# First two tiles' values loaded as two pieces per partition, the memory's rows from GpSimd's queue

## The chip, the cores and the metric

One core of a Trainium2 chip runs the whole program. The metric is device time of one execution in microseconds (us), measured without a profile; the kernel before was run three times, and one more execution was profiled. The engines are named as in the profile: PE (TensorE's matmuls), PEld (its weight loads), DVE (VectorE), ACT (ScalarE), POOL (GpSimd), SP (SyncE, which only issues DMAs here).

## What is computed

Chunked attention with memory rows, and then two dense layers one after the other. Shapes: 4 batches, 8 heads, 768 positions, head width 64; that is 3072 tokens of 512 values; the hidden width is 2048. Inputs and result are float32.

```python
for c in range(24):                       # chunks of 32 queries
    k_ctx = k[:, :, max(0, 32*c-16) : min(S, 32*c+32+8)]
    k_full = concat(mem_k (8 rows), k_ctx);  v_full = concat(mem_v (8 rows), v_ctx)
    a = softmax(q_c @ k_full.T / 8)       # 64 keys for each query
    out[:, :, c] = a @ v_full
x = out as [3072, 512]
h = x @ w_in;   x = (h * clip(h + 3, 0, 6) / 6) @ w_out          # first layer
h = x @ w_in2;  x = (h if h>=1, 0 if h<=-1, else (h+1)**2/4) @ w_out2   # second
```

## The kernel before

**Tiling.** Tokens go in six tiles of 512 (T). Attention goes in 24 value blocks of four chunks (128 queries), s = 0 to 23, so blocks 0 to 3 feed the first tile and 4 to 7 the second. Queries and keys are loaded in blocks of three chunks (j), values per block s as one tile `v_sb` of 128 partitions by 2 by 512 for s < 8: chunk c of the block has partitions 32c to 32c+31, and its 64 value rows (8 of the memory, 56 of the context) lie as rows 0 to 31 in the first half and 32 to 63 in the second. Each dense product is done in three matmuls of 512 columns (high by high, high by low, low by high part), lines L603 to L605 for the hidden product (tile `ph`), L652 to L654 and L657 to L659 for the projection. The weights come packed (`raw`, 512 KB each, issued at L279) and are unpacked by ACT and DVE into `w` (L286 to L312).

**Attention of a block.** Scores on PE (L460), maximum on DVE, exponentials on ACT (L485), normalising and a transpose on DVE (L495, L504), values on PE (L529), and the split of the result into a high part on ACT and a low part on DVE (L575, L579). The hidden products of the first tile read the blocks 0 to 3 whole, so the first `ph` matmul comes after the values of block 3.

**What sets the order.** Nothing is ordered by hand. `Plan.run` (L136) is a list scheduler: every task has a key, a duration table entry (such as `("SP", 430)`), reads, writes and a buffer from a pool; the planner picks the task that can start soonest by its own clock, and within 100 ns of that the one of the lowest key. The instructions are then written out engine by engine in the order of the planned starts, so on the chip each engine runs that fixed list, waiting where an input isn't there. SP's list is the DMA issues.

**Fillers.** Where the plan leaves PE idle before 60 us, lines L752 to L769 put matmuls of the constant `warm` tile (bfloat16) into a buffer that the next task will overwrite anyway:

```python
while at + ns <= t.start + more:
    P.matmul(c, warm, warm[:, :n].unsqueeze(1).to_broadcast([128, m, n]), ...)
    at += ns
```

They have the line L765. How many stand in a gap is decided by the plan's times, with 2.4 columns to the nanosecond; they then run whether or not the gap is there.

**Values' loads.** `load_values` (L385) cuts each block into runs of consecutive rows, one DMA each from SP: about 8 or 9 for each of the blocks 0 to 7, of 8, 24, 32, 64 or 96 rows. For j < NEARLY the source is the array `qkv`, in which queries, keys and values of a block j lie side by side; for later j it is `qk` and `vv`. Each DMA from SP signals on one of eight semaphores in turn, and a DMA waits until the one eight places before it has landed.

Of the kernel before, what the change touches and what calls it, by code (L numbers as in the profile page):

```python
# [22 lines left out]
NMEM = 8  # L23
CHUNK, LEFT, RIGHT = 32, 16, 8
# [7 lines left out]
NC = DM // 128  # L32
NF = DFF // 128
GRP = 4
NEARLY = 6
LATE_W = GRP * (QB + KB)
T = 512
NT = NTOK // T
# [38 lines left out]
class Plan:  # L77
# [58 lines left out]
    def run(self, at):  # L136
        free = dict(at)
        bw = 0
        last_kind = None
        ready = {e: [] for e in free}  # L140

        def put(t):
            for e, _ in t.ways:
                ready[e].append(t)

        for t in self.tasks:
            if not t.left:
                put(t)
        left = len(self.tasks)
        order = []  # L150
        while left:
            best = None
            for e, ts in ready.items():
                found = []
                blocked = set()
                for t in sorted(ts, key=lambda t: (t.key, t.n)) if e == "SP" else ts:
                    est = max(free[e], t.ready)
                    taken = [] if blocked & {p for b in t.bufs if not b.slot for p in b.pools} else self.slots_for(t)
                    if taken is None or len(taken) < sum(b.slot is None for b in t.bufs):
                        if e == "SP":  # L160

                            blocked.update(p for b in t.bufs if b.slot is None for p in b.pools)
                        continue
                    found.append((max([est, *(s.at + HOP for s in taken)]), t))
                if not found:
                    continue
                first = min(x[0] for x in found)
                if e == "PE" and last_kind:

                    same = [x for x in found if x[1].kind and x[0] <= free[e] + WINDOW]  # L170
                    found = same or found
                est, t = min(
                    (x for x in found if x[0] <= first + WINDOW), key=lambda x: (x[1].key, x[1].n)
                )
                if best is None or est < best[0]:
                    best = est, e, t
            assert best, ("no task can start", [
                (t.n, t.emit.__qualname__, t.key, [b.name for b in t.bufs if b.slot is None])
                for ts in ready.values() for t in ts][:20])
            est, e, t = best  # L180
            for x, _ in t.ways:
                ready[x].remove(t)
            ns = dict(t.ways)[e]
            if e == "PE":
                ns += CHANGE * (bool(t.kind) != bool(last_kind))
                last_kind = t.kind
            t.eng, t.start = e, est
            free[e] = est + ns
            t.end = est + ns + TAIL[e]
            if t.kb:  # L190
                bw = max(bw, t.end + 1900) + t.kb / 0.39
                t.end = bw
            for b, s in zip([b for b in t.bufs if b.slot is None], self.slots_for(t)):
                b.slot, s.used = s, True
            for b in t.bufs:
                b.users -= 1
                b.free_at = max(b.free_at, t.end)
                if not b.users:
                    b.slot.used, b.slot.at = False, b.free_at
            for d in t.then:  # L200
                d.left -= 1
                d.ready = max(d.ready, est)
                if not d.left:
                    put(d)
            for d in t.next:
                d.left -= 1

                alone = all(x == e for x, _ in d.ways)
                d.ready = max(d.ready, est + ns if alone else t.end + HOP)
                if not d.left:  # L210
                    put(d)
            order.append(t)
            left -= 1
        order.sort(key=lambda t: (t.start, t.n))
        return order
# [11 lines left out]
def fused_kernel(ctx: ExitStack, tc: tile.TileContext, qkv, qk, vv, wpk, const, out):  # L227
# [40 lines left out]
    def weight(l, f, z, key, after=()):  # L268
# [43 lines left out]
            eng.tensor_tensor(out=t[:, 1], in0=words()[2], in1=t[:, 0], op=ALU.subtract)  # L312

        lo, hi = (raw, "lo"), (raw, "hi")
        add(("SP", 430), key - 4, load, writes=[lo, hi], kb=512, after=after)
        add([("DVE", dve(512, True)), ("ACT", 575)], key - 0.5, shift, writes=[lo])
        add(("ACT", 575), key - 0.5, rebase, writes=[hi])
        add(("DVE", dve(512)), key - 0.4, sign, [hi], [lo])
# [21 lines left out]
    def wide(j):  # L340
        return j * NCH >= 2 * T // CHUNK

    def load_block(j, key):

        early = key < 0

        over = key > 1.75 * NF
        far = 3 * (not early)  # L350
        w = KB + KC if wide(j) else KB
        q = q_buf[j] = Buf(
            ["in"] + ["w"] * ((early or over) and not wide(j)), [128, NP * (QB + w)], F32, "q_sb",
            **({"w": 1} if early else {}),
        )
        if j < NEARLY:
            src = qkv[j, :, :WQ]
        else:
            src = qk[2 * (j - NEARLY):2 * (j - NEARLY) + 2].rearrange("g d w -> (g d) w")
        after = last_w if over else ()  # L360
        if not wide(j):
            add(("SP", 430), key - 6 - far, lambda e: nc.sync.dma_start(tile_of(q), src), writes=[(q, 0)], kb=448, after=after, line="load")
            return
        k4 = lambda: tile_of(q)[:, NP * QB:].rearrange("p (a t) -> p a t", a=NP)
        add(
            ("SP", 430), key - 6 - far, lambda e: nc.sync.dma_start(
                k4()[:, :, :KB], src[:, NP * QB:].rearrange("p (a t) -> p a t", a=NP)
            ), writes=[(q, 1)], kb=256, after=after, line="load",
        )
        add(  # L370
            ("SP", 430), key - 6 - far, lambda e: nc.sync.dma_start(tile_of(q)[:, :NP * QB], src[:, :NP * QB]),
            writes=[(q, 0)], kb=192, after=after, line="load",
        )

        def spread(e):
            k = k4()
            cast(e, k[:, :, KB + NMEM:], k[:, :, NMEM + CHUNK:KC + CHUNK])
            cast(
                e, k[:, :, 2 * CHUNK:2 * CHUNK + 2 * KC].rearrange("p a (b t) -> p a b t", b=2)[:, :, :, :NMEM],
                k[:, :, :NMEM].unsqueeze(2).to_broadcast([128, NP, 2, NMEM]),  # L380
            )

        add([("DVE", 330), ("ACT", 400)], key - 4.5, spread, [], [(q, 1)])

    def load_values(s, key):  # L385
# [4 lines left out]
        v = v_buf[s] = Buf(  # L390
            ["lv"] + ["w"] * early, [128, 2, H * D], F32, "v_sb", **({"w": 1} if early else {}),
        )
        runs = []
        for c in range(NSB):
            j, i = divmod(s * NSB + c, NCH)
            cuts = [0] + [NMEM] * (i > 0) + [CHUNK] * (not late) + [KC]
            for a, b in zip(cuts, cuts[1:]):
                row = a if b <= NMEM else a + CHUNK * i
                p, col = (64 * (c % 2) + a, c // 2) if late else (CHUNK * c + a % CHUNK, a // CHUNK)
                for r in runs:  # L400
                    if r[0] == j and r[1] + r[4] == row and r[2] + r[4] == p and r[3] == col:
                        r[4] += b - a
                        break
                else:
                    runs.append([j, row, p, col, b - a])
        for n, (j, row, p, col, m) in enumerate(sorted(runs, key=lambda r: (r[3], r[2]))):
            if j < NEARLY:
                src, rows = qkv[j, row:row + m, WQ:], lambda t: t
            else:
                g = 2 * (j - NEARLY)  # L410
                src, rows = vv[g:g + 2, row:row + m, :].rearrange("g k c -> k g c"), lambda t: t.rearrange("k (g c) -> k g c", g=2)
            add(
                ("SP", 430), key - 5 - 3 * (not early),
                lambda e, src=src, rows=rows, p=p, m=m, col=col: nc.sync.dma_start(rows(tile_of(v)[p:p + m, col]), src),
                writes=[(v, n)], kb=2 * m, line="load v",
            )
        v.parts = len(runs)

    def block(s, key):
        first = key < 0  # L420
# [89 lines left out]
        def values(e, m=None):  # L510
# [23 lines left out]

        qs = sorted({j for j, _ in places})
        add(
            ("PE", 750 if all(wide(j) for j in qs) else 1450), key - 4, scores,
            [(q_buf[j], x) for j in qs for x in range(1 + wide(j))],
            [(sc[0], 0), (sc[1], 0)], hold=[st], line="scores", kind="a",
        )  # L540
# [6 lines left out]
            add(("ACT", 1150), key - 3, lambda e, h=h: exps(e, h), [(sc[h], 0), (sm, 2)], [(st, h), (sm, 0, h)])  # L547
        add(("DVE", 280), key - 2.5, weigh, [(sm, 0, 0), (sm, 0, 1)], [(sm, 3)])
        add(("DVE", dve(512)), key - 2.4, norm, [(sm, 3)], [(st, 0), (st, 1)])
        of_v = [(v, n) for n in range(v.parts)]  # L550
        if late:
            for c in chunks:
                for b in range(2):
                    add(("DVE", dve(256)), key - 2.2, lambda e, c=c, b=b: turn_part(e, c, b), [(st, 0), (st, 1)], [(tr, c, b)])
            ts = [(tr, c, b) for c in chunks for b in range(2)]
            add(("PE", 750), key - 1, values, [*ts, *of_v], [(x, 0) for x in pv], line="values", kind="a")
        else:
            add(("DVE", 635), key - 2.2, turn, [(st, 0), (st, 1)], [(tr, 0)])
            for m in range(2):
# [128 lines left out]
    def second_x(n):  # L688
        xhi, xlo = xbuf[NT + n]
        key = NK + NF * n  # L690
        for c in range(NC):
            x = Buf(["in", "o", "st"], [128, T], F32, "x2raw")
            add(
                ("SP", 430), key - 8 + 0.5 * c, lambda e, c=c, x=x: nc.sync.dma_start(tile_of(x), ymid[n, :, c]),
                [("ymid", n, c)], [(x, 0)], kb=256, after=[h_tasks[key - NF]],
            )
            ways = [("ACT", act(T)), ("DVE", dve(T, True))]
# [138 lines left out]
```

## Time and profile before

| | us |
|---|---|
| median of 3 runs | 1161.72 (1161.0 to 1162.23) |
| the profiled execution, its own time | 1161.94 |
| its span, first to last instruction | 1160.1 |
| PE busy in the span | 1144.1 |
| DVE, ACT, POOL busy | 614.9, 457.8, 0.2 |

The time of an execution holds 1.84 us that lie outside the span. PE is busy nearly throughout, and what it does after the first tile's attention is a fixed list of matmuls; the first 60 us look different. In the trace a float32 matmul counts as two (the order has 64 for the values of a block, the trace 128). A wait is put down to what ended it; "issue" means that the engine waited for nothing that the profile shows.

### The profile page before, as it was taken

To read this page: it belongs to the slowest core of one execution; us is meant where nothing else is said; L and a number is where in the kernel's file an instruction comes from. 1 tells how busy PE (TensorE), PEld (TensorE's weight loads), DVE (VectorE), ACT (ScalarE), POOL (GpSimd) and SP (SyncE) were. 2 spreads that over 40 slices of the span, in tenths; PEclk is the share of its full clock that TensorE was granted. 3 is DMA by queue.
4 is the path that set the end of the run, shared out by engine and by line. 5 is a ranking of instruction groups with operands and counts; after the bars stand their busy time and mean duration, and the time that the engine had idled before them with its cause. 6 is when DMAs were issued, how large, how long until landed. Compare 5 with 4: busy or idle time off the path is not lost.

```text
span 1160.1 us, 20860 instructions
## 1 busy us (share of the span) xinstructions
PE 1144.1 (99%) x8766; PEld 939.5 (81%) x8766; DVE 614.9 (53%) x1116; ACT 457.8 (39%) x1083; POOL 0.2 (0%) x4
## 2 busy tenths in 40 slices
PE   8899999999999999999999999999999999999998
PEld 6687888888887888888888888888888888888887
DVE  2589955445555445643899634434434434433433
ACT  3599633334333333333788423223223223222221
POOL 0000000000000000000000000000000000000000
PEclk8699999999999999999999999999999999999999
DMA  6791131112112112210656300200200200000100
GB/s 207 249 396 55 57 100 35 51 54 90 48 35 87 51 51 74 70 38 19 200 183 216 91 1 1 73 1 1 73 1 1 73 1 1 37 1 1 37 1 37
DMA packets 48644, 81.05 MB, mean 70 GB/s; under 512 B 5158, under 2 KB 28582, under 8 KB 48550
## 3 DMA queue, kind: packets, MB, share of 16 engines
q1 hardware_dynamic: 48550, 79.71, 20.9%
q8 instruction: 69, 1.13, 0.4%
q14 instruction: 25, 0.20, 0.1%
HBM read 67.11 MB, written 12.58 MB: 69 GB/s over the span
## 4 chain that ended last, share of the span: by engine, by line
PE 97%; DMA 1%; issue 1%; ACT 1%; DVE 0%; SPq 0%; DVEq 0%; ACTq 0%
PE ph L603 15%; PE ph L604 15%; PE ph L605 15%; PE py L652 8%; PE po L657 8%; PE po L659 8%; PE po L658 8%; PE py L653 7%; PE py L654 7%; PE sc L460 2%; PE pv L529 2%; PE pv L519 1%; PE pv L765 1%; DMA ymid<-ysb 0%; DMA v_sb<-qkv 0%
## 5 line engine op out<-in xcount | busy, mean ns | idle before, releaser
L603 PE MATMUL ph<-xhi,w 128*128 128x512 f32 x768 | 300.5, 391 | 0.0
L604 PE MATMUL ph<-xlo,w 128*128 128x512 f32 x768 | 299.2, 390 | 0.0
L605 PE MATMUL ph<-xhi,w 128*128 128x512 f32 x768 | 299.0, 389 | 0.0
L626 ACT ACTIVATE r<-r,bias 128x512 f32<-128x512 f32 x96 | 69.3, 722 | 286.6 <-DVE r L623 286.6
L633 DVE TENSOR_TENSOR glo<-r,ghi 128x512 fp32r<-128x512 f32 x192 | 132.6, 690 | 81.9 <-ACT ghi L632 80.4
L632 ACT CAST ghi<-r 128x512 fp32r<-128x512 f32 x192 | 119.5, 623 | 133.7 <-DVE r L629 71.2
L603 PEld LDWEIGHTS ph<-xhi,w 128*128 128x128 f32 x768 | 144.5, 188 | 30.5 <-ACT raw L286 0.3
L605 PEld LDWEIGHTS ph<-xhi,w 128*128 128x128 f32 x768 | 144.3, 188 | 30.2
L604 PEld LDWEIGHTS ph<-xlo,w 128*128 128x128 f32 x768 | 144.5, 188 | 29.7
L652 PE MATMUL py<-ghi,w 128*128 128x512 f32 x384 | 153.5, 400 | 1.3 <-DVE ysb L679 1.3
L654 PE MATMUL py<-ghi,w 128*128 128x512 f32 x384 | 149.8, 390 | 0.0
L653 PE MATMUL py<-glo,w 128*128 128x512 f32 x384 | 149.8, 390 | 0.0
L657 PE MATMUL po<-w,ghi 128*128 128x512 f32 x384 | 149.4, 389 | 0.0
L658 PE MATMUL po<-w,ghi 128*128 128x512 f32 x384 | 149.4, 389 | 0.0
L659 PE MATMUL po<-w,glo 128*128 128x512 f32 x384 | 149.4, 389 | 0.0
L619 DVE SCALAR_TENSOR_TENSOR r<-r,ph 128x512 f32<-128x512 f32 x96 | 65.8, 685 | 154.0 <-ACT r L616 153.3
L623 DVE TENSOR_SCALAR r<-ph 128x512 f32<-128x512 f32 x96 | 66.3, 691 | 152.2 <-PE ph L605 152.2
L616 ACT ACTIVATE r<-ph,bias 128x512 f32<-128x512 f32 x96 | 66.2, 689 | 191.9 <-PE ph L605 191.9
L629 DVE TENSOR_TENSOR r<-ph,r 128x512 f32<-128x512 f32 x96 | 66.3, 690 | 74.7 <-ACT r L626 74.7
L652 PEld LDWEIGHTS py<-ghi,w 128*128 128x128 f32 x384 | 72.0, 188 | 18.4 <-DVE ysb L679 1.7
L654 PEld LDWEIGHTS py<-ghi,w 128*128 128x128 f32 x384 | 72.1, 188 | 15.2
L659 PEld LDWEIGHTS po<-w,glo 128*128 128x128 f32 x384 | 72.1, 188 | 15.0
(52 smaller groups left out, 962.7 us busy)
## 6 DMA issues: line engine op xcount, KB each, us to landing
raw<-wpk SPq DMA_DIRECT2D x64, 512.0 KB
ymid<-ysb SPq DMA_DIRECT2D x24, 256.0 KB
x2raw<-ymid SPq DMA_DIRECT2D x24, 256.0 KB
out<-osb SPq DMA_DIRECT2D x24, 256.0 KB
q_sb<-qk SPq DMA_DIRECT2D x21, 256.0 KB
v_sb<-vv SPq DMA_DIRECT2D x43, 112.0 KB
q_sb<-qk SPq DMA_DIRECT2D x21, 192.0 KB
v_sb<-vv SPq DMA_DIRECT2D x24, 128.0 KB
```

The lines of the kernel that those rows point to most:

```text
L603: P.matmul(p, whi[:, c, :], xh[:, c, :], start=(c == 0), stop=False)
L604: P.matmul(p, whi[:, c, :], xl[:, c, :], start=False, stop=False)
L605: P.matmul(p, wlo[:, c, :], xh[:, c, :], start=False, stop=(c == NC - 1))
L626: add(("ACT", act(T) + 100), k + 0.35, lambda e: A.activation(out=rt(), in_=rt(), func=AF.Square, bias=bias[:, 1:2], scale=0.5,), [], [(r, ...
L632: add(("ACT", act(T)), k + 0.5, lambda e: A.copy(tile_of(ghi), rt()), [(r, 0)], [(ghi, 0)])
L633: add(("DVE", dve(T)), k + 0.6, lambda e: V.tensor_tensor(out=tile_of(glo), in0=rt(), in1=tile_of(ghi), op=ALU.subtract,), [(r, 0), (ghi, ...
L652: P.matmul(y, w2hi, gh, start=first, stop=False)
L653: P.matmul(y, w2hi, gl, start=False, stop=False)
L654: P.matmul(y, w2lo, gh, start=False, stop=last)
L657: P.matmul(y, gh[:, t], wt[:, 0], start=first, stop=False)
L658: P.matmul(y, gh[:, t], wt[:, 1], start=False, stop=False)
L659: P.matmul(y, gl[:, t], wt[:, 0], start=False, stop=last)
```

## The change

The values of blocks 0 to 7 are loaded with one DMA for each chunk whose memory rows and context rows lie next to each other in the source (the first chunk of a block j: 32 partitions, two pieces of 512 values each), and with two for the others: 24 partitions with two pieces from SP, and 8 partitions (the memory's rows and eight context rows) with two pieces from GpSimd's queue. NEARLY goes from 6 to 11, so that all of these blocks are read from `qkv`. Besides, numbers in the planner's tables change: 430 to 450 for a DMA issue from SP, 800 for a later value load (whose key keeps its place), 750 to 800 for later scores, 750 to 1070 for later values, 337 to 450 for a partial transpose, and a rule for the landing of a DMA from GpSimd.

```diff
-NEARLY = 6
+NEARLY = 11
@@ Plan.run
             if t.kb:
                 bw = max(bw, t.end + 1900) + t.kb / 0.39
-                t.end = bw
+                t.end = bw if e == "SP" else t.end + 1900 + t.kb / 0.1
@@ load_values
+        if not late:
+            v.parts = []
+            for c in range(NSB):
+                j, i = divmod(s * NSB + c, NCH)
+                for a, b, row, step, way in (
+                    ((0, CHUNK, 0, CHUNK, ("SP", 500)),) if i == 0 else (
+                        (NMEM, CHUNK, CHUNK * i + NMEM, CHUNK, ("SP", 500)),
+                        (0, NMEM, 0, CHUNK * (i + 1), ("POOL", 550)),
+                    )
+                ):
+                    rows = qkv[j, row:row + b - a, WQ:]
+                    src = bass.AP(rows.tensor, rows.offset, [rows.ap[0], [step * rows.ap[0][0], 2], rows.ap[1]])
+                    part = (v, c, a)
+                    v.parts.append(part)
+                    add(
+                        way, key - 5, lambda e, src=src, p=CHUNK * c + a, n=b - a:
+                        (nc.gpsimd if e == "POOL" else nc.sync).dma_start(tile_of(v)[p:p + n], src),
+                        writes=[part], kb=5.6 * (b - a), line=way[0] + "load v",
+                    )
+            return
-            cuts = [0] + [NMEM] * (i > 0) + [CHUNK] * (not late) + [KC]
+            cuts = [0] + [NMEM] * (i > 0) + [KC]
-                ("SP", 430), key - 5 - 3 * (not early),
+                ("SP", 800), key - 8,
@@ block
-            ("PE", 750 if all(wide(j) for j in qs) else 1450), key - 4, scores,
+            ("PE", 800 if all(wide(j) for j in qs) else 1450), key - 4, scores,
-                    add(("DVE", dve(256)), key - 2.2, lambda e, c=c, b=b: turn_part(e, c, b), [(st, 0), (st, 1)], [(tr, c, b)])
+                    add(("DVE", 450), key - 2.2, lambda e, c=c, b=b: turn_part(e, c, b), [(st, 0), (st, 1)], [(tr, c, b)])
-            add(("PE", 750), key - 1, values, [*ts, *of_v], [(x, 0) for x in pv], line="values", kind="a")
+            add(("PE", 1070), key - 1, values, [*ts, *of_v], [(x, 0) for x in pv], line="values", kind="a")
```

SP's list at the program's start, of the kernel before: the first two blocks of queries and keys (`q_sb`), the values of block 0 (`v_sb`), and the third `q_sb`.

```order
L362 DMA q_sb<-qkv 128x896 x2
L414 DMA v_sb<-qkv 32x512
L414 DMA v_sb<-qkv 8x512
L414 DMA v_sb<-qkv 24x512
L414 DMA v_sb<-qkv 8x512
L414 DMA v_sb<-qkv 24x512
L414 DMA v_sb<-qkv 32x512
L414 DMA v_sb<-qkv 96x512
L414 DMA v_sb<-qkv 32x512
L362 DMA q_sb<-qkv 128x896
```

The same place of the changed kernel:

```order
L363 DMA q_sb<-qkv 128x896 x2
L412 DMA v_sb<-qkv 32x2x512
L412 DMA v_sb<-qkv 24x2x512 x2
L412 DMA v_sb<-qkv 32x2x512
L363 DMA q_sb<-qkv 128x896
```

Eight issues of values became four; two pieces of 8 partitions went to POOL's list, which holds 21 such DMAs in all and nothing else. The first `raw` is the 41st DMA of SP's list before and the 23rd now.

SP's list of the kernel before from the last values of block 3 on: the first packed weights (`raw`), the next `q_sb`, and the values of block 4.

```order
L414 DMA v_sb<-qkv 96x512
L414 DMA v_sb<-qkv 32x512
L279 DMA raw<-wpk 128x512 x2
L362 DMA q_sb<-qk 128x896
L279 DMA raw<-wpk 128x512 x2
L414 DMA v_sb<-qkv 8x512
L414 DMA v_sb<-qkv 24x512
```

The same place of the changed kernel:

```order
L412 DMA v_sb<-qkv 24x2x512 x2
L412 DMA v_sb<-qkv 32x2x512
L280 DMA raw<-wpk 128x512 x2
L363 DMA q_sb<-qkv 128x896
L280 DMA raw<-wpk 128x512 x6
L363 DMA q_sb<-qkv 128x896
L280 DMA raw<-wpk 128x512 x2
L412 DMA v_sb<-qkv 24x2x512 x2
L412 DMA v_sb<-qkv 32x2x512
L412 DMA v_sb<-qkv 24x2x512
L280 DMA raw<-wpk 128x512 x6
```

Ten weight loads now stand ahead of the values of block 4 where four stood, and six more between these and block 5's. Block 4's values go into the buffer of block 0's, block 5's into that of block 1's, in both kernels.

PE's list of the kernel before around the values of block 0 (L529; L765 are fillers, L460 the scores of block 2):

```order
L765 MATMUL pv<-warm 128x128
L765 LDWEIGHTS warm
L765 MATMUL pv<-warm 128x128
L529 MATMUL pv<-tr,v_sb 64x32 x64
L460 MATMUL sc<-q_sb 32x8 x6
L460 MATMUL sc<-q_sb 32x56 x2
```

The same place of the changed kernel (L552 are the values of block 0; the scores ahead of them, L483, are those of block 2):

```order
L483 MATMUL sc<-q_sb 32x64 x2
L483 MATMUL sc<-q_sb 32x56 x4
L552 MATMUL pv<-tr,v_sb 64x32 x64
L788 LDWEIGHTS warm
L788 MATMUL sc<-warm 128x256
```

The scores run one block further ahead, and the fillers stand in other gaps. Counted over the lists, up to and just behind the first `ph` matmul, whose place among the real work is the same (five blocks of scores and four of values stand ahead of it):

| fillers (columns each) | before | now |
|---|---|---|
| ahead of scores 0 | 26 (256) | 27 (256) |
| ahead of scores 1 | 15 (256) | 16 (256) |
| other gaps, up to values 3 | 11 (256), 145 (128) | 47 (256), 7 (128) |
| ahead of the first `ph` | 8 (512) | 10 (512) |
| behind the first 12 `ph` matmuls | 17 (256) | 15 (512) |

PE's list after the values of block 7 is the same in both kernels.

## Rows read from the trace of the kernel before

**Rows 1.** The page: engines' busy time, and the queue of kind "instruction".

```profile
PE 1144.1 (99%) x8766; PEld 939.5 (81%) x8766; DVE 614.9 (53%) x1116; ACT 457.8 (39%) x1083; POOL 0.2 (0%) x4
...
q8 instruction: 69, 1.13, 0.4%
```

**Rows 2.** Two stretches: each engine's busy time (instructions), granted clock, DMA share, GB/s.

```profile
0.00:55.00 55.00, 44.17 (x1246) 36.50 (x1247) 22.40 (x64) 23.14 (x98) 0.20 (x4) 0.74 0.70 226
...
60.00:1160.00 1100.00, 1094.91 (x7496) 899.04 (x7494) 588.41 (x1046) 430.32 (x966) 0.00 (x0) 1.00 0.19 61
```

**Rows 3.** PE's waits in the whole span: total us, times, longest.

```profile
PE pv L529 <- issue: 4.5, 2, 2.9
PE sc L460 <- issue: 4.1, 4, 1.9
PE py L652 <- DVE ysb L679: 1.3, 1, 1.3
...
PE sc L460 <- DMA q_sb<-qkv: 0.8, 1, 0.8
```

**Rows 4.** PE in order of time, from 11 to 59 us: start, us, what, count.

```profile
11.19 0.37 PE L460 MATMUL sc<-q_sb 64*32 64x8 f32 x26 [0.33 <-issue]
...
19.13 1.02 PE L460 MATMUL sc<-q_sb 64*32 64x56 f32 x62 [1.90 <-issue]
...
24.66 2.20 PE L529 MATMUL pv<-tr,v_sb 32*64 32x32 f32 x74 [1.58 <-issue]
26.79 1.46 PE L765 MATMUL sc<-warm 128*128 128x256 bf16 x6
28.18 0.91 PE L460 MATMUL sc<-q_sb 64*32 64x8 f32 x47
30.51 0.96 PE L460 MATMUL sc<-q_sb 64*32 64x64 f32 x49 [1.41 <-issue]
...
39.55 1.38 PE L460 MATMUL sc<-q_sb 64*32 64x8 f32 x82 [0.50 <-issue]
40.86 3.49 PE L765 MATMUL pv<-warm 128*128 128x128 bf16 x42
44.28 0.30 PE L529 MATMUL pv<-tr,v_sb 32*64 32x32 f32 x3
47.52 3.37 PE L529 MATMUL pv<-tr,v_sb 32*64 32x32 f32 x125 [2.95 <-issue]
...
52.24 2.74 PE L765 MATMUL ph<-warm 128*128 128x512 bf16 x6 [0.38 <-issue]
54.42 0.99 PE L603 MATMUL ph<-xhi,w 128*128 128x512 f32 x1
...
58.39 2.03 PE L765 MATMUL sc<-warm 128*128 128x256 bf16 x17
```

**Rows 5.** The DMA queues from 39.55 to 45.05 us, then from 45.05 to 47.52.

```profile
q1 hardware_dynamic: 527, 1.86, 97.6%
...
q8 instruction: 1, 0.02, 2.5%
```

**Rows 6.** Three stretches, columns as in rows 2.

```profile
39.55:45.10 5.55, 5.02 (x127) 4.67 (x128) 3.98 (x8) 2.86 (x7) 0.00 (x0) 0.70 0.98 339
...
24.66:28.08 3.42, 3.42 (x80) 2.79 (x80) 0.97 (x4) 2.93 (x19) 0.00 (x0) 0.50 0.77 250
19.13:22.10 2.97, 2.97 (x101) 2.63 (x104) 0.93 (x3) 0.00 (x0) 0.00 (x0) 0.50 0.98 310
```

**Rows 7.** SP's issues in order of time: start, us, line, count.

```profile
1.65 4.13 SPq L414 DMA_DIRECT2D v_sb<-qkv  x8
...
24.45 0.91 SPq L279 DMA_DIRECT2D raw<-wpk  x2
...
41.98 11.01 SPq L414 DMA_DIRECT2D v_sb<-vv  x9
53.03 7.83 SPq L279 DMA_DIRECT2D raw<-wpk  x11
```

**Rows 8.** Line L414 up to 62 us: one issue's ns, least, median, most.

```profile
L414 SPq DMA_DIRECT2D v_sb<-qkv x39: 288/317/1577, 1.7 to 35.4; - x39
```

More of the change, by code (lines that the diff above doesn't have):

```diff
@@ L314, in weight @@
         lo, hi = (raw, "lo"), (raw, "hi")
-        add(("SP", 430), key - 4, load, writes=[lo, hi], kb=512, after=after)
+        add(("SP", 450), key - 4, load, writes=[lo, hi], kb=512, after=after)
         add([("DVE", dve(512, True)), ("ACT", 575)], key - 0.5, shift, writes=[lo])
@@ L361, in load_block @@
         if not wide(j):
-            add(("SP", 430), key - 6 - far, lambda e: nc.sync.dma_start(tile_of(q), src), writes=[(q, 0)], kb=448, after=after, line="load")
+            add(("SP", 450), key - 6 - far, lambda e: nc.sync.dma_start(tile_of(q), src), writes=[(q, 0)], kb=448, after=after, line="load")
             return
@@ L365, in load_block @@
         add(
-            ("SP", 430), key - 6 - far, lambda e: nc.sync.dma_start(
+            ("SP", 450), key - 6 - far, lambda e: nc.sync.dma_start(
                 k4()[:, :, :KB], src[:, NP * QB:].rearrange("p (a t) -> p a t", a=NP)
@@ L370, in load_block @@
         add(
-            ("SP", 430), key - 6 - far, lambda e: nc.sync.dma_start(tile_of(q)[:, :NP * QB], src[:, :NP * QB]),
+            ("SP", 450), key - 6 - far, lambda e: nc.sync.dma_start(tile_of(q)[:, :NP * QB], src[:, :NP * QB]),
             writes=[(q, 0)], kb=192, after=after, line="load",
@@ L395, in load_values @@
             j, i = divmod(s * NSB + c, NCH)
-            cuts = [0] + [NMEM] * (i > 0) + [CHUNK] * (not late) + [KC]
+            cuts = [0] + [NMEM] * (i > 0) + [KC]
             for a, b in zip(cuts, cuts[1:]):
                 row = a if b <= NMEM else a + CHUNK * i
-                p, col = (64 * (c % 2) + a, c // 2) if late else (CHUNK * c + a % CHUNK, a // CHUNK)
+                p, col = 64 * (c % 2) + a, c // 2
                 for r in runs:
@@ L416, in load_values @@
             )
-        v.parts = len(runs)
+        v.parts = [(v, n) for n in range(len(runs))]
     def block(s, key):
@@ L549, in block @@
         add(("DVE", dve(512)), key - 2.4, norm, [(sm, 3)], [(st, 0), (st, 1)])
-        of_v = [(v, n) for n in range(v.parts)]
+        of_v = v.parts
         if late:
@@ L693, in second_x @@
             add(
-                ("SP", 430), key - 8 + 0.5 * c, lambda e, c=c, x=x: nc.sync.dma_start(tile_of(x), ymid[n, :, c]),
+                ("SP", 450), key - 8 + 0.5 * c, lambda e, c=c, x=x: nc.sync.dma_start(tile_of(x), ymid[n, :, c]),
                 [("ymid", n, c)], [(x, 0)], kb=256, after=[h_tasks[key - NF]],
```

## The prediction

> **What bounds the kernel now.** I read the page first, then stretches, then PE's waits, and last PE in order of time beside the DMA queues. The page has PE busy for 99% of the span [rows 1]. The stretches show that this holds from 60 us on, where PE misses 5 of 1100 us, while in the first 55 us it is busy for 44.2 at a mean clock of 0.74, and much of that busy time is fillers [rows 2]. The real dense work starts at 54.42 us, right behind eight fillers that are really a wait [rows 4]. Behind that point PE's list is fixed and nearly without gaps, so whatever the first `ph` matmul gains or loses is carried to the end. The change is priced by that one instant.
>
> PE's waits in the whole span hold no wait for values and only 0.8 us for queries and keys [rows 3]: the loads that the change makes fewer were not what PE waited for. The largest entries are "issue", 4.5 and 4.1 us. In order of time these stalls stand at a fixed spacing: from the one that ends at 24.66 to the one at 30.51 there are 74 + 6 + 47 = 127 matmuls, from 39.55 to 47.52 there are 82 + 42 + 3 = 127, from there to 52.24 125 + 2 = 127 (two of the eight fillers) [rows 4]. With its weight load each is two instructions, so a stall comes every 254; and the queue of kind "instruction" carried 69 packets, which over PE's 2 x 8766 instructions is one for 254 [rows 1]. I read this as PE's instruction fetch: one packet brings the next block of 127 matmuls, and is asked for when the block before it begins.
>
> When does it come? PE entered a block at 39.55. Until 45.05 the DMA engines were 97.6% busy with 1.86 MB of data and no instruction packet started; it started after that, and PE went on at 47.52 [rows 4, 5]. So the fetch stood 5.5 us behind data that SP had issued already, and needed 2.4 us more. The interval from stall to stall was 8.0 us there, 5.9 from 24.66, with a DMA share of 0.77 in its first 3.4 us, and 5.5 from 19.13, with 0.98 in its first 3.0 [rows 4, 6].
>
> [...]
>
> **The change, part by part.** *SP's issues.* Blocks 0 to 3 lose 34 - 16 = 18 issues. Eight took 4.13 us before, and the first weights were issued at 24.45, as the 41st DMA [rows 7]. Now they are the 23rd; an issue of two pieces is not in the trace, so I bound it by 0.29 and 1.58 us and take 0.5, nearer to the median and to 4.13 / 8 [rows 7, 8]: first weights at about 0.7 + 22 x 0.5 = 12 us (7 to 35 by the bounds). On PE's path this gives nothing by itself, as PE didn't wait for these loads.
>
> *GpSimd's pieces.* Ten for the first tile, on an engine that was busy for 0.2 us [rows 1]. Their cost isn't in the trace; below nothing is excluded, since they replace SP issues that PE didn't wait for; above, at 1.58 us each as SP's slowest, all ten are out by 18 us, and block 3's values were used from 44.28 on [rows 4, 8]. I take nothing. If that cover went, the first use is the values of block 0, and each us of lateness there would cost one.
>
> *Fewer fillers.* Up to the first `ph` 107 stand where 205 stood: 98 x 2 instructions less, 0.77 of a block. From 11.19, where a block begins, PE had eight further block starts up to 52.24: 41.05 us, 5.13 each [rows 4]. The count to that first boundary is nearly the same now (223 matmuls), and 924 remain instead of 1022: seven blocks, and then 25 matmuls of values and the ten fillers of 512 columns.
>
> *Denser loads beside the fetch.* The bytes stay the same but come sooner. Queries, keys and values of the first tile are 4.8 MB; with ten `raw` and two `q_sb` right behind them SP has 11 MB to issue that wait for no values of PE's, where before it had 4.8 MB, then 2.6 MB from 24.45 on, and then sat in small loads (11.01 us for nine from 41.98, with weights behind them at 53.03) [rows 7]. At the 339 GB/s of the densest stretch [rows 6] 11 MB fill the engines to about 33 us. The next wait of SP's is at block 4's values, for PE to finish block 0's; behind it queue six `raw`, block 5's values and sixteen `raw`. Nobody needs block 4's values soon, but these weights, once released, stand ahead of the fetch again. So six of the seven blocks see the engines full. I price these with the mean of the three intervals measured with data ahead of the packet, (8.0 + 5.9 + 5.5) / 3 = 6.45 us, and the seventh, the block of 23 fillers after SP's wait, with 5.1. Start: sooner by nothing, 11.3. Last boundary: 11.3 + 6 x 6.45 + 5.1 = 55.1. Then 25 matmuls of values, 0.76 us at 2.20 / 74, and ten fillers at 2.74 / 6, the pace behind the stall that ended at 52.24, twice as long for a column as at 58.39: 4.6 us [rows 4]. First `ph` at 60.4 instead of 54.4, later by 6.0.
>
> *Fillers behind the first `ph`.* 17 x 256 columns took 2.03 us [rows 4]; 15 x 512 are 1.76 times as many columns: 3.6, later by 1.5. Weights can't be what ends last there, as they arrive earlier than before and PE never waited for them [rows 3].
>
> *Table numbers.* They change only the plan; after block 7's values PE's list is the same: nothing.
>
> Sum: 6.0 + 1.5 = 7.5 on a span of 1160.1, 1167.6; with the 1.84 us outside it 1169.4 for this execution, which lay 0.2 above the median of 1161.72. Since stalls overlap partly with waits for ACT and DVE that I can't add up exactly, I round down: 1168.5, slower by 0.6%.
>
> **The rivals.** *The fetch is no slower than before.* Seven blocks at 5.13: last boundary 11.3 + 35.9 = 47.2, first `ph` at 52.6, earlier by 1.8, less 1.5 behind it: 1161.4, no change. For it: two of three intervals are near 5.5. Against it: 8.0 in the one stretch where weights were dense.
>
> *The fetch doesn't wait for data any more than for its own 2.4 us.* Then PE's own work decides: 41.05 less some 8.6 of stalls [rows 3, 4], less 98 fillers at 3.49 / 42 = 8.1, is 24.3; last boundary 35.6, first `ph` near 40, and 1149 in all. Real gain is likely a part of it, as values then wait for ACT's exponentials: 1149 to 1159, middle 1156. Against it: rows 5. [...] The 5.5 us of rows 5 speak against so short a wait.
>
> *The fetch stands behind everything outstanding.* SP may have eight DMAs in flight; eight `raw` are 4.2 MB, 12.4 us at 339 GB/s, plus 2.4. Two such blocks at 14.8 instead of 6.45 add 17: 1185. It decides if the fetch's wait has no limit below SP's eight.
>
> *Values late from GpSimd.* If each piece took 3 us and landed behind dense data, block 3's would still be there at 40; only block 0's could be late, by some 5 us: 1166, and this instead of the fetch.
>
> *The change doesn't do what it says*, fewer issues from SP: the order shows that it does.
>
> **How the numbers follow.** A difference below 0.2%, 2.3 us, can't be told from none here. Forecast (1164 to 1177 as its own range): 0.52. Fetch as before, with a stall or a filler gap more or less: 0.20, of which 0.14 lie within 0.2%, 0.04 below, 0.02 above. Fetch free of the data: 0.20. Fetch behind everything: 0.06. Late pieces: 0.02. That makes faster 0.24, same 0.14, slower 0.62. The range leaves out the best part of the free fetch and the worst of the last: 1154 to 1180.
>
> **What would show it.** First `raw` issued near 12 us, and a DMA share over 0.9 from 3 us to about 33. Seven more issue stalls after the one near 11 us, 127 matmuls apart, most intervals over 6 us; the instruction packets late in them. First `ph` near 60 us, and the distance from it to the end longer by 1.5 us. No wait of PE for `v_sb`. I am wrong if the first `ph` comes before 54 us, if intervals stay near 5 us with the DMA engines full, or if PE waits for GpSimd's pieces.

## The result and the profile after

The changed kernel takes 1174.64 us (median of 4 runs, 1172.4 to 1176.28); the kernel before took 1161.45 beside it (1161.0 to 1162.23). The ratio is 1.0112, 95% interval 1.009 to 1.0134: slower by 1.1%. The prediction was 1168.5, within 1154 to 1180. The profiled execution took 1176.14 us with a span of 1174.4, so it is one of the longer runs of this kernel; the one before had 1160.1.

The page of the changed kernel, the lines that answer to [rows 1], and the queue that GpSimd now uses:

```profile
PE 1144.7 (97%) x8666; PEld 935.6 (80%) x8666; DVE 614.3 (52%) x1111; ACT 461.4 (39%) x1088; POOL 12.0 (1%) x25
...
q8 instruction: 68, 1.11, 0.4%
q0 software_dynamic: 672, 0.69, 0.3%
```

PE is busy as long as before, 1144.7 us for 1144.1, though its list has 98 fillers fewer ahead of the first `ph`. The span grew by 14.3 us. Cut at the first `ph` (columns as in [rows 2]):

```profile
0.00:67.27 67.27, 43.94 (x1147) 32.99 (x1148) 21.32 (x61) 22.59 (x97) 9.22 (x20) 0.65 0.99 291
67.27:1174.00 1106.73, 1100.73 (x7521) 902.65 (x7519) 593.00 (x1051) 438.82 (x992) 2.78 (x5) 1.00 0.17 56
```

Up to the first `ph` it is 67.27 us in place of 54.42, 12.85 more; behind it, to the end of the span, 1107.1 in place of 1105.7, 1.4 more. The DMA engines are full (0.99) for the whole first part, where they were at 0.70 [rows 2]. PE's waits in the span, for [rows 3]:

```profile
PE pv L552 <- issue: 10.8, 4, 4.1
PE sc L483 <- issue: 9.6, 3, 4.4
PE ph L788 <- ACT st L508: 2.2, 1, 2.2
PE sc L483 <- DMA q_sb<-qkv: 1.3, 1, 1.3
...
PE ph L788 <- DVE xlo L602: 0.7, 1, 0.7
PE py L675 <- DVE ysb L702: 0.3, 1, 0.3
```

The "issue" entries went from 8.6 to 20.4 us, and nothing waits for `v_sb`. In order of time, for [rows 4]:

```profile
9.76 0.25 PE L483 MATMUL sc<-q_sb 64*32 64x8 f32 x8
11.28 0.96 PE L483 MATMUL sc<-q_sb 64*32 64x8 f32 x76 [1.28 <-DMA q_sb<-qkv]
16.63 0.54 PE L483 MATMUL sc<-q_sb 64*32 64x8 f32 x28 [4.39 <-issue]
...
24.47 0.54 PE L483 MATMUL sc<-q_sb 64*32 64x8 f32 x28 [2.92 <-issue]
...
30.97 1.07 PE L552 MATMUL pv<-tr,v_sb 32*64 32x32 f32 x30 [3.43 <-issue]
...
37.52 0.43 PE L483 MATMUL sc<-q_sb 64*32 64x56 f32 x6 [2.29 <-issue]
...
45.08 0.43 PE L552 MATMUL pv<-tr,v_sb 32*64 32x32 f32 x8 [4.10 <-issue]
...
56.56 0.73 PE L552 MATMUL pv<-tr,v_sb 32*64 32x32 f32 x17 [2.92 <-issue]
...
61.66 1.06 PE L552 MATMUL pv<-tr,v_sb 32*64 32x32 f32 x26 [0.32 <-issue]
63.41 4.42 PE L788 MATMUL ph<-warm 128*128 128x512 bf16 x10 [0.70 <-DVE xlo L602]
67.27 0.99 PE L626 MATMUL ph<-xhi,w 128*128 128x512 f32 x1
```

From 16.63 to 61.66 the trace has 888 matmuls of PE in seven blocks (128, 126, 128, 126, 254 for two, 126), 127 each in the mean; at 51.52 a boundary passes with no stall. One interval beside the DMA queues, as in [rows 5]: from 16.63 to 21.40 us with no instruction packet, then from 21.40 to 24.47.

```profile
q1 hardware_dynamic: 433, 1.08, 93.2%
```

```profile
q1 hardware_dynamic: 275, 0.67, 102.8%
q8 instruction: 1, 0.02, 2.8%
```

The instruction packet started 4.8 us after PE entered the block ahead of the one that the packet brings. Read out of the trace for each boundary, that delay is 4.8, 4.0, 4.0, 4.8, 3.7, 2.3 and 2.1 us here, mean 3.7; in the kernel before, for the boundaries from 11.19 to 47.52, it is 1.7, 1.2, 3.0, 3.4, 2.4, 0.7, 5.5 and 2.1, mean 2.5. SP's issues, for [rows 7]:

```profile
15.01 5.19 SPq L412 DMA_DIRECT2D v_sb<-qkv  x4
20.25 0.90 SPq L280 DMA_DIRECT2D raw<-wpk  x2
...
50.14 20.96 SPq L280 DMA_DIRECT2D raw<-wpk  x16
```

The first `raw` went out at 20.25, 4.2 us sooner than before, not at 12.

### The profile page after: what moved, and what is told of

The parts are those of the page before. It is cut to its first block, busy times and chain, and to the rows that moved or that the text cites. A ratio compares the mean times of both kernels' runs of the same rounds, so it can differ in the third digit from the quotient of the medians.

```text
span 1174.4 us, 20687 instructions
## 1 busy us (share of the span) xinstructions
PE 1144.7 (97%) x8666; PEld 935.6 (80%) x8666; DVE 614.3 (52%) x1111; ACT 461.4 (39%) x1088; POOL 12.0 (1%) x25
## 3 DMA queue, kind: packets, MB, share of 16 engines
q8 instruction: 68, 1.11, 0.4%
## 4 chain that ended last, share of the span: by engine, by line
PE 96%; issue 2%; DMA 1%; DVE 0%; ACT 0%; SPq 0%; DVEq 0%; ACTq 0%
PE ph L626 15%; PE ph L627 15%; PE ph L628 15%; PE py L675 8%; PE po L680 7%; PE po L682 7%; PE po L681 7%; PE py L676 7%; PE py L677 7%; PE pv L552 2%; PE sc L483 2%; PE pv L542 1%; PE sc L788 1%; DMA q_sb<-qkv 1%; PE ph L788 1%
```

## The experiments

Each ratio is to the kernel before, run beside it on the same chip; the runs of one kernel (4 to 19) lie 1 to 8 us apart. Three chips were used for the experiments; on them the kernel before had medians of 1162.58, 1162.12 and 1163.67 us. Kernels are compared over chips by their ratios. The first `ph` is that of the one profiled execution.

| kernel | first `ph`, us | median, us | ratio (95%) |
|---|---|---|---|
| before | 54.42 | 1161.45 | 1 |
| after | 67.27 | 1174.64 | 1.0112 (1.009 to 1.0134) |
| after, memory rows from SP | 62.16 | 1174.08 | 1.0095 (1.0067 to 1.0123) |
| after, a block in one load | 62.17 | 1173.07 | 1.0090 (1.0061 to 1.0119) |
| after, fillers cut in two | 69.65 | 1179.61 | 1.0149 (1.0114 to 1.0183) |
| after, no fillers | 61.22 | 1169.46 | 1.0044 (1.0023 to 1.0065) |
| one load, weights held | 52.58 | 1169.68 | 1.0063 (1.0039 to 1.0086) |
| one load, no fillers | 52.23 | 1162.50 | 0.9996 (0.9985 to 1.0007) |
| one load, held, no fillers | 43.86 | 1156.38 | 0.9951 (0.9931 to 0.997) |
| before, new numbers alone | 53.14 | 1162.40 | 1.0000 (0.9987 to 1.0013) |
| before, no fillers | 50.04 | 1155.84 | 0.9945 (0.9925 to 0.9966) |
| before, held, no fillers | 47.59 | 1157.86 | 0.9952 (0.9934 to 0.9969) |

**Is it the loads or the planner's numbers?** The loads as before, with the new numbers:

```diff
-("SP", 430)   ("PE", 750)   ("DVE", dve(256))   ("PE", 750)    # issue, scores, transpose, values
+("SP", 450)   ("PE", 800)   ("DVE", 450)        ("PE", 1070)   # late values' load: ("SP", 800)
```

> The kernel before with the planner's new numbers alone (450 for a DMA, 800 and 1070 for the late scores and values, 450 for a late transpose, 800 for a late values' load), every load as before. Theory, the loss is the loads of the first two tiles: 1159 to 1163, first ph at 53.5-55. Rival, the numbers' new order costs it (the +9.5 us behind the first ph apart from the loads): 1166 to 1172.

1162.4 us, ratio 1.0000, first `ph` at 53.14: the loss is in the loads of the first two tiles and the order that the planner makes of them. The new order with the old loads was not tried.

**GpSimd's queue.** The pieces that GpSimd issues, from SP at the same places of the plan:

```diff
-(nc.gpsimd if e == "POOL" else nc.sync).dma_start(tile_of(v)[p:p + n], src)
+nc.sync.dma_start(tile_of(v)[p:p + n], src)
```

> The changed kernel, with the pieces of the memory's rows issued by SP at the same places of the plan instead of by GpSimd. In the changed kernel the first tile's loads ran at about 200 GB/s from 5 to 20 us with every engine of the DMA shown busy, and PE's first block after the scores of block 0 came at 16.6 us instead of 11.2. If GpSimd's queue is what slows them (its packets in turn with SP's), the rate in that stretch rises to 330 to 380 GB/s, the second block starts near 12 us and the time falls to about 1169. If the narrow loads themselves (8, 24 or 32 partitions, two pieces each) are what is slow, the rate stays near 200 to 250 and the time at 1172 to 1178.

1174.08 us: the same as after. The rate of the first loads, from 5 to 20 us, stays low as well. Columns as in [rows 2]; the kernel before, after, this one, and the next experiment's, in this order:

```profile
5.00:20.00 15.00, 11.97 (x521) 10.47 (x519) 5.99 (x19) 6.02 (x37) 0.00 (x0) 0.97 0.58 166
```

```profile
5.00:20.00 15.00, 9.33 (x248) 6.90 (x246) 3.51 (x11) 4.37 (x29) 2.03 (x4) 0.79 1.03 205
```

```profile
5.00:20.00 15.00, 9.82 (x253) 7.28 (x251) 3.51 (x11) 5.15 (x33) 0.00 (x0) 0.74 0.74 183
```

```profile
5.00:20.00 15.00, 10.74 (x378) 8.20 (x379) 3.75 (x12) 5.16 (x33) 0.00 (x0) 0.88 1.02 405
```

With GpSimd's queue the engines are full for 205 GB/s, without it 0.74 busy for 183. From 5 to 20 us its own packets take 10.7% of the engines' time for 0.29 MB, and SP's 92.1% for 2.77 MB, where without it SP's take 72.6% for 2.72 MB. The profile without them has the first `ph` 5 us sooner, but it is the shortest of that kernel's runs (1172.23) and the profile of after one of its longest; the medians differ by 0.6 us and the ratios by 0.0017, 2 us, less than a kernel's runs vary. The queue is not the cause of the 1.1%; a part of up to some 3 us can't be excluded. In the profiles the queue does delay the first fetch. With it PE entered a block at 7.45 us, the packet started at 13.58, and the second block began at 16.63; without it the packet started 0.8 us after PE entered that block, and the second began at 13.8, though the third `q_sb` was later (2.70 us of PE's wait for 1.28).

**A block in one load.** The values of each of the blocks 0 to 7 laid out in a further array, and one DMA of 128 partitions by 4 KB in place of six or seven loads; plan and order unchanged.

```diff
-(nc.gpsimd if e == "POOL" else nc.sync).dma_start(tile_of(v)[p:p + n], src)   # each piece
+nc.sync.dma_start(tile_of(v).rearrange("p b w -> p (b w)"), v8[s])            # the first alone
```

> The changed kernel with the plan as it is, but the values of each of the blocks 0 to 7 in one DMA of 128 partitions by 4 KB from an array laid out so. Same bytes, three SP issues less per block, none from GpSimd. If narrow loads are what is slow, the first tile's 4.9 MB are in by about 15 us (rate over 330 GB/s from 5 to 15), the first weights are issued before 13 us, the stall at the second block ends near 12 us, and the time falls by 4 to 6 us to 1168 to 1171; it does not fall to 1161, because the weights then stand ahead of the instruction fetch all the sooner (intervals of 6 to 7 us stay). If the rate is set by something else (the row pitch, the bytes themselves), it stays near 1174. If the fetch theory is wrong and PE waits for data, it goes to 1160 or below.

1173.07 us, 2 us over the upper end of the range, with the first `ph` 5.1 us sooner in the profiles. Of that 5.1 the spans keep 2.5: behind the first `ph` PE waits 2.2 us for `ysb` here, 0.3 in after. The rate doubled to 405 GB/s. Weights, issued from 7.61 us on, are a part of that; from 5 to 8 us, nearly all with queries, keys and values, it was 392:

```profile
5.00:8.00 3.00, 3.00 (x111) 2.31 (x109) 0.30 (x3) 0.00 (x0) 0.00 (x0) 1.00 1.01 392
```

So the low rate belongs to the many loads of few partitions. Whether to their packets, or to the small amount that eight outstanding ones of them hold, no run here tells. With full engines from 5 us on, PE's stalls became regular:

```profile
13.10 0.53 PE L490 MATMUL sc<-q_sb 64*32 64x8 f32 x28 [2.69 <-issue]
19.29 0.38 PE L490 MATMUL sc<-q_sb 64*32 64x8 f32 x28 [1.56 <-issue]
25.45 1.06 PE L559 MATMUL pv<-tr,v_sb 32*64 32x32 f32 x29 [3.28 <-issue]
31.72 0.31 PE L490 MATMUL sc<-q_sb 64*32 64x56 f32 x6 [2.02 <-issue]
38.02 0.43 PE L559 MATMUL pv<-tr,v_sb 32*64 32x32 f32 x6 [3.84 <-issue]
```

6.2 us from stall to stall, whatever PE has to do in between: the fetch sets the pace. For the four intervals between them the packet starts 3.6 to 3.8 us after PE enters the block ahead, and PE goes on 2.4 to 2.6 us after that. (At the boundary at 38.02 it starts after 1.7 us, with the engines 0.66 busy until then.)

**Fillers as blocks to be fetched.** Each filler behind the first 27 cut into two of half the columns: 80 matmuls more for the same columns.

```diff
-P.matmul(c, warm, warm[:, :n]...to_broadcast([128, m, n]))
+for g in range(2):
+    P.matmul(c[:, g * m // 2:(g + 1) * m // 2], warm, warm[:, :n]...to_broadcast([128, m // 2, n]))
```

> The changed kernel with every filler behind the first 27 cut into two of half the columns: the same columns on PE, 80 matmuls more ahead of the first hidden product (and 15 more behind its first twelve). The theory of the instruction fetch: 80 of 127 matmuls are 0.63 of a block, at 6.4 us a block 4 us more: 1177 to 1180, and one more stall ahead of the first hidden product, still 127 matmuls apart. The rival, that the stalls are waits for data or for buffers and stand where they stand: same time, 1174.6 plus or minus 1, stalls at the same instructions as before.

1179.61 us, 5.0 over after by the medians and 4.3 by the ratios, as expected. From the second block's start to the first `ph` it is 54.6 us (15.04 to 69.65) in place of 50.6 (16.63 to 67.27): 4.0 more, the expected figure; the first `ph` comes only 2.4 later, as the second block began 1.6 sooner in this profile. Eight stalls stand ahead of the first `ph`, where in after there were seven, and the last is of 3.07 us, where in after it was 0.32:

```profile
54.32 2.21 PE L552 MATMUL pv<-tr,v_sb 32*64 32x32 f32 x79 [4.31 <-issue]
56.46 0.39 PE L790 MATMUL pv<-warm 128*128 128x64 bf16 x4
56.78 1.49 PE L552 MATMUL pv<-tr,v_sb 32*64 32x32 f32 x43
61.34 0.85 PE L552 MATMUL pv<-tr,v_sb 32*64 32x32 f32 x21 [3.07 <-issue]
```

Behind the first `ph` the two profiles differ by 0.4 us only. The fillers' own time on PE is the same, 0.39 us for four of 64 columns as for two of 128 in after: the 4.0 us more come with 80 matmuls more, at the same columns.

**No fillers behind the first 27, in after.** `FILL` is the planned time in ns up to which gaps are filled.

```diff
-FILL = 60000
+FILL = 7000
```

> The changed kernel without any filler behind the first 27: 80 matmuls less ahead of the first hidden product and 15 less behind its first twelve. Fetch theory: 844 matmuls from the second block on are 6.65 blocks, the last boundary near 16.6 + 6 x 6.4 = 55, the first hidden product near 58.5 instead of 67.8, and 3.4 to 5.6 us less behind it: about 1161 to 1164. Rival, that fillers cost only their own columns where PE is waiting anyway: they go into the waits, and the gain is the ten before and the fifteen behind, 5 to 8 us: 1166 to 1169. Second rival, that they keep the clock up: slower than 1174.

1169.46 us, 5.5 us over the range of the theory of fetched blocks and 0.5 over the rival's: 5.2 us gained by the medians. (Two of its ten runs took 1162.69 and 1163.57, the others 1167.67 to 1170.92; the profile is of one of the others.) The granted clock was 0.50 from 10 to 64 us, in which PE was busy for 23.94 us (columns as in [rows 2]):

```profile
10.00:30.00 20.00, 7.37 (x346) 6.56 (x346) 5.94 (x17) 6.19 (x39) 1.67 (x3) 0.50 1.01 257
30.00:64.00 34.00, 16.57 (x597) 14.95 (x598) 13.05 (x34) 13.01 (x50) 1.67 (x3) 0.50 1.03 323
```

The first `ph` came at 61.22, not at 58.5, as the stalls stayed (14.6 us of issue waits in front of the values alone) and a block took 6.9 us, not 6.4 (six from 16.40 to 57.76). Behind it nothing was gained, though 15 fillers were gone there (1106.9 us for 1107.1): the granted clock was still 0.69 from 66 to 70 us and 0.89 from 70 to 74 (a `ph` matmul took 0.63 us up to 70.1 and 0.39 from 71.2 on), where in after it was 1.00 from 71 on. How much of the miss is the clock's was not tried.

**The same without the change.** `FILL = 7000` in the kernel before.

> The kernel before, without the fillers behind the first 26. Theory of the fetched blocks: some 180 matmuls fewer are 1.4 blocks of 127 fewer to fetch ahead of the first ph, at 5.1 us each (the mean interval in the kernel before), so first ph moves from 54.4 to 46-48 us if the weights are there, and no later than 53 us if the tenth weight (ready at 52.9 there) holds it: 1153 to 1160. Rival, the fillers' clock is worth as much as their blocks cost (as in the changed kernel without fillers, where half a clock until 64 us left only 5 us of a gain): first ph at 50-54 with the granted clock at 0.50 until then, 1161 to 1165.

1155.84 us, ratio 0.9945 (0.9925 to 0.9966): faster than both kernels, in the range of the theory of fetched blocks, though the first `ph`, at 50.04, came only 4.4 us sooner and not at 46 to 48. The clock was 0.50 here too, from 10 to 50 us, and did not take the gain back:

```profile
10.00:50.00 40.00, 21.47 (x936) 19.64 (x936) 17.68 (x48) 16.75 (x84) 0.00 (x0) 0.50 0.74 248
```

The fillers kept up the clock in this stretch (0.70 from 10 to 50 us in the kernel before) and cost more than that gave. Whether they cost it by their instructions or by their own time on PE this run doesn't tell; for the changed kernel the halved fillers above show that instructions cost by themselves (4.3 to 5.0 us for 80 matmuls more at the same columns).

**Weights held.** One load for a block, and the first weights' loads behind two held by a DVE memset of one word that is planned behind the low part of block 0, 1, 2 or 3 (two weights each); the weights' loads keep their order.

```diff
+if l == 0 and 2 <= 2 * f + z < 10:
+    gates.append(add(("DVE", 70), key - 4.1, lambda e: V.memset(one word of raw), writes=[lo, hi]))
-add(("SP", 450), key - 4, load, writes=[lo, hi], kb=512, after=after)
+add(("SP", 450), key - 4, load, writes=[lo, hi], kb=512, after=after, line="raw" if l == 0 else None)
```

> One load of 128 partitions for each block's values, and the weights' loads behind the first two held until a block of the attention is done (a one-word memset on DVE that each of the next eight needs; the loads stay in their order). Theory, a fetch of instructions stands behind the transfers that SP has outstanding: with SP's queue no longer full of weights from 15 us on, the intervals between PE's stalls fall from 6.2 us to 5.1 or less, first ph comes at 54-57 us (62.2 with the same loads and no hold), and the time at 1165 to 1169. Rival, the fetch takes 6 us whatever is outstanding: the intervals stay at 6.2, first ph at 62-65, 1173 to 1176. Rival, the weights become late: the stalls go, but ph waits for w, 1170 to 1175.

The DMA engines' share from 19 to 46 us fell from 0.99 to 0.44, and the stalls thinned out:

```profile
22.86 1.07 PE L565 MATMUL pv<-tr,v_sb 32*64 32x32 f32 x29 [1.85 <-issue]
...
32.41 0.43 PE L565 MATMUL pv<-tr,v_sb 32*64 32x32 f32 x6 [1.88 <-issue]
...
41.62 0.32 PE L565 MATMUL pv<-tr,v_sb 32*64 32x32 f32 x8 [2.40 <-issue]
...
48.29 4.79 PE L806 MATMUL ph<-warm 128*128 128x512 bf16 x11 [1.13 <-DVE raw L320]
52.58 0.72 PE L643 MATMUL ph<-xhi,w 128*128 128x512 f32 x1
...
60.77 8.17 PE L806 MATMUL ph<-warm 128*128 128x512 bf16 x24 [4.95 <-ACT st L521]
```

From the boundary at 22.86 to the one at 41.62 there are four blocks, two of whose ends pass without a stall: 18.76 / 4 = 4.7 us a block, where it was 6.2. At 41.62 PE entered a block with nothing outstanding from SP. The DMA queues from 41.65 to 42.75 us, then to 43.5:

```profile
DMA packets 0, 0.00 MB, mean 0 GB/s; under 512 B 0, under 2 KB 0, under 8 KB 0
```

```profile
q8 instruction: 1, 0.02, 9.7%
```

The packet started 1.15 us after the boundary; at 22.86 and 32.41, where no data packet started before it either, 1.46 and 1.11. At 37.13, with two weights outstanding, it took 2.3 us (37.13 to 39.40), and the weights' last landings were then 38.5 and 39.9. That is the fetch behind data, shown by its delay without data and with: 1.1 to 1.5, 2.3, and 3.6 to 3.8 us with SP's queue full (the case above; 3.6 here too, at 12.85, ahead of the held loads). The first `ph` came 9.6 us sooner than with the same loads unheld (52.58 for 62.17), sooner than expected. But of that some 3 us are left in the time (ratio 1.0063 for 1.0090, whose intervals overlap), and 1169.68 is 0.7 over the theory's range. Behind the first `ph`, PE now waits 4.95 us for ACT's exponentials of the fifth block, which stand on ACT and DVE between the weights' unpacking, where it waited 2.20. The larger part is fillers again: the new plan has 24 behind this wait for 15, and they take 8.17 us, with the granted clock at 0.63 from 61 to 68.5, for 3.40. The same place with the loads unheld:

```profile
68.36 3.40 PE L795 MATMUL ph<-warm 128*128 128x512 bf16 x15 [2.20 <-ACT st L515]
```

**Held or not, without fillers.**

> One load of 128 partitions for each block's values and no fillers behind the first 27; the weights are not held. It completes a table of four: fillers and weights as planned 1173.1, weights held 1169.7, weights held and no fillers 1156.4. If weights ahead of the fetch cost time by themselves (6.2 us between stalls in place of 4.5): the last of some 6.6 blocks comes 8 to 11 us later than with the weights held, 1162 to 1167. Rival, without fillers the start is bound by the attention's own chain and the weights cost nothing: 1155 to 1159.

> As the kernel with the weights held, and no fillers behind the first 27. If the fetch behind outstanding transfers was what held the start, and the fillers' blocks the rest: first ph at 46-50 us, 1157 to 1163, less than before. Rival, the half clock takes it back: first ph at 52-56, 1164 to 1169.

One load and no fillers: ratio 0.9996, in the theory's range. Here the fetch sets the pace throughout. Blocks begin at 12.07, 18.19, 24.26, 30.30, 36.50, 42.64 and 48.82, 6.0 to 6.2 apart, and each packet starts 3.6 to 3.7 us after PE enters the block ahead (read out of the trace), though PE is busy for less than half of the stretch, at a granted clock of 0.50:

```profile
12.07:48.82 36.75, 17.27 (x764) 15.98 (x764) 13.94 (x40) 12.28 (x65) 0.00 (x0) 0.50 1.03 408
```

At 408 GB/s 3.7 us are 1.5 MB, an estimate from this row: as much as about three of the weights' loads passes ahead of the packet, not all eight that may be outstanding. Held as well: 0.9951 (0.9931 to 0.997), 1156.38 us, a little under its range. The weights that SP sends early cost 0.45% by themselves, some 5 us; here the intervals don't overlap. The first `ph` moved by 8.4 (52.23 to 43.86), and the same wait, 2.2 us in the one and 4.97 in the other, gave 2.8 of that back:

```profile
43.86 0.79 PE L643 MATMUL ph<-xhi,w 128*128 128x512 f32 x1 [1.13 <-DVE raw L320]
...
53.67 0.80 PE L643 MATMUL ph<-xhi,w 128*128 128x512 f32 x1 [4.97 <-ACT st L521]
```

**The kernel before, held, no fillers.**

> The kernel before with its own loads, no fillers behind the first 26, and the weights held as in the two kernels with held weights. Theory of the fetch behind outstanding transfers: first ph at 43 to 47 us in place of 50.0, and 1151 to 1154, the fastest here. Rival, what comes sooner is given back where ph waits for ACT's exponentials of the fifth block (5.0 us in the other kernel with held weights and no fillers): 1155 to 1158, the same as with fillers taken away alone.

1157.86 us, ratio 0.9952, the rival's range and the same as without fillers alone (0.9945); the 1151 to 1154 of the theory of the fetch did not come. The first `ph` came at 47.59, 2.5 us sooner; here the trace has no wait of PE for ACT behind it as long as 5 us but 2.6 us for `st` in the scores, 0.5 with the weights unheld, which gives 2.1 of the 2.5 back. Three kernels, by different ways, end at ratios of 0.9945 to 0.9952, with their first `ph` between 43.86 and 50.04: there the start is no longer bound by the fetch alone. Which of the waits on ACT and DVE bounds it was not tried.

## Why the prediction was right in sign, and 6 us short

*PE's first stretch decides, the rest is fixed.* Right: 12.85 of the 14.3 us lie ahead of the first `ph`.

*Stalls every 127 matmuls are fetches, one block ahead, behind data that SP has issued.* Right, and now shown rather than read: by the packet's delay of 1.1 to 1.5 us with nothing outstanding against 3.6 to 3.8 with SP's queue full, by the time that held weights give, and by what 80 more matmuls cost for the same columns. At the boundary at 41.62 with held weights the packet started 1.15 us after it, with PE at work in the block ahead, and no issue stall followed up to the first `ph`; in after the issue waits are 20.4 us.

*Start of the second block at 11.3, "sooner by nothing".* This is the term that was mis-sized: 16.63, by 5.3 us of the 6.9 that the first `ph` came later than the 60.4 of the sum. Two steps failed. I expected full engines from 3 us on, but left the first fetch at its old delay without a reason; my own 6.45 us from 7.45, where PE entered the block ahead, would have put the boundary at 13.9 and the sum near 1171. And the densest stretch of before, 339 GB/s, was a stretch of weights, whose rate I gave to loads of 8 to 32 partitions. They ran at 205 GB/s with the engines full, and so the third `q_sb` was late (1.28 us of PE's wait), and the fetch stood behind them: the packet started at 13.58. With a block's values in one load the same boundary passed at 13.10, and without GpSimd's queue at 13.8.

*Seven blocks, six at 6.45 and one at 5.1, 43.8 us.* Right in sum: 61.66 - 16.63 = 45.0. In part that is luck. The intervals were 7.8, 6.5, 6.6, 7.6, 6.4, 5.0 and 5.1, and the two short ones had the engines full as well. The mean of three unequal intervals of before came near the 6.2 us per block of the regular case above.

*The tail ahead of the first `ph`, 5.4 us.* Right: 5.6, of which 0.7 is a wait for `xlo`.

*Fillers behind the first `ph`, 1.5 us.* Right in size (1.4 of the span), in part by luck. The 15 fillers take 3.40 us for 2.03, as forecast, but they stand behind a wait for ACT's exponentials of 2.2 us that I had not seen, and a wait for `ysb` that fell from 1.3 to 0.3 us gave a part of that back:

```profile
73.03 3.40 PE L788 MATMUL ph<-warm 128*128 128x512 bf16 x15 [2.20 <-ACT st L508]
```

*First weights at 12 us.* Wrong, 20.25: in the traces of before and after an issue of SP waits until the DMA eight places before it has landed, and these landed slowly. Four issues took 5.19 us, 1.3 each, where I had taken 0.5; of that 3.4 us are one wait, at 18.7, for the `q_sb` issued at 7.94, eight places before, and 0.8 three waits for `v_sb`. The engines were full in any case, with the values' loads in place of weights, and so it changed the sum only by way of the first boundary.

*GpSimd's pieces at nothing, and the table numbers at nothing.* The numbers are at nothing (ratio 1.0000). The pieces are at 0 to some 3 us in the time; no value was waited for, and what they cost in the profiles stands at the first fetch (second block at 16.63 with them, 13.8 without).

*The rivals.* "Fetch no slower than before" is out: 3.7 us mean delay for 2.5. "Fetch free of data" is out by the same rows, and by delays that grow with what is outstanding: 1.1 to 1.5 us with nothing, 2.3 with two weights, 3.6 to 3.8 with SP's queue full. "Behind everything outstanding" is out as well: SP's eight loads of 512 KB are 10 us at the 405 GB/s of 5 to 20 us, an estimate, and in the kernel with full engines from 5 us on the packet came 4.0 us after the boundary at most. It passes behind a part of them only. "Late GpSimd pieces" is out: no wait for `v_sb`.

## What to carry to other kernels

Where stalls marked "issue" return after a fixed number of instructions, here 127 matmuls with their weight loads, look for an instruction fetch: count the instructions between two of them, and look when the instruction queue's packet starts. Loads that nobody waits for can still cost: here prefetched weights ahead of the fetch cost 5 us. So can fillers: the kernel before is 6 us faster without them (ratio 0.9945), and in the changed one 80 matmuls more for the same columns cost 4 us. Price a mechanism in every part of a kernel that has its conditions: here the first fetch was left out of the sum, and the second block began at 16.63, not 11.3. When the start of a program is made faster, look what gets late next, since of 9.6 us won at the first `ph` some 3 arrived at the end.

## What the runs showed of the hardware that was not expected

- A stretch of mostly loads of 8 to 32 partitions in two pieces ran at 183 to 205 GB/s (5 to 20 us); with values in loads of 128 partitions by 4 KB it was 392 (5 to 8 us).
- With GpSimd's queue in use beside SP's the DMA engines were 1.03 busy for 205 GB/s; with SP alone 0.74 for 183.
- The packet with the instructions of 127 matmuls started 1.1 to 1.5 us after the boundary on idle DMA engines and mostly 3.6 to 3.8 us on engines full of 512 KB loads, but 4.0 at most with values in one load, less than the 10 us of the estimate above for all of SP's eight.
- Without fillers the kernel before had a granted clock of 0.50 from 10 to 50 us, up to its first `ph`, and was faster than with them (1155.84 us for 1162.12).
